# Spectral layers on one core: the place of an older group's inverse, and of its copy, in the middle stage

## The chip, the cores and the metric

The kernel runs on one core of a Trainium2 chip. The metric is the device time of one execution in microseconds (us), over several runs: before the change the median of three is 1185.11 us (1184.79 to 1185.26). The profile shows one further execution.

The engines are named as in the profile: PE is TensorE (PEld is its loading of weights), ACT is ScalarE, DVE is VectorE, POOL is GpSimd, SP is SyncE. ACTq and SPq are the queues from which an engine issues DMAs.

## The reference

A row of 2048 positions by 576 channels goes through four layers. Layers A are Fourier mixing: layer norm, a DFT over the channels and one over the sequence, the real part of it, and a residual. Layers B are an H3 block: layer norm, then a gate that is a long causal convolution along the sequence, done by FFT for each channel.

```
def A(x): a, b = x @ Wd_re.T, x @ Wd_im.T          # 576 x 576
          return Ws_re @ a - Ws_im @ b              # 2048 x 2048
def B(q): kv = shift_conv(k, 4 taps) * v
          y = irfft(rfft(kv, 4096) * rfft(ssm_k, 4096))[:2048] + kv * ssm_D
          return q * y
x = x + A(norm(x)); x = x + B(norm(x)); x = x + A(norm(x)); x = x + B(norm(x))
```

The convolution `y` doesn't depend on `x`, so the kernel computes it once and uses it in both B layers.

## The kernel before, in words

Matrices are held as two float32r parts, a high and a low one, and a product is three matmuls: high by high, high by low, low by high. What splits a value into its parts is a copy on ScalarE (the high part, rounded) and a subtraction on VectorE (the low part).

*The two halves of the first 600 us.* The first A layer is the function `layer`: 128 steps, of 14 matmuls of 512 columns each ("s" and "rm" in the profile, four full accumulators and one for the remaining columns), over a matrix of which 128x512 pieces arrive by DMA and are split (lines 99 and 100, "mats"). When two groups of 16 steps are done, the four or five accumulators are copied out (`evac_u`, `evac_r`), and the product with the channel DFT follows for four row blocks (`hidden`, "bk<-w,u": blocks of 27 matmuls of 288 columns; VectorE adds the result to the residual at line 289). The convolution is a generator, `branch`, that is woven in between these matmuls. It has a first stage (the outer part of the FFT), the **middle stage** with which the change deals, and a last one (`i2_products`, the outer part of the inverse FFT).

*The middle stage.* There are 64 groups (two channel halves by 32). For group g:

- `mid_kernel` (line 522): three matmuls of 288 columns, the "kernel trio", into a bank; then three ScalarE copies (lines 524 to 526) that lay out the kernel's spectrum in one of two tiles `kk`.
- `mid_signal` (529): the "signal trio" into a bank; then VectorE's lines 532 to 535 make the complex product with the spectrum, in place, in the `kk` tile.
- `mid_round` (538): the product is split into `yf` (two tiles), a rounding on ScalarE and a subtraction on VectorE (line 520, 128x288).
- `mid_inverse` (543): the "inverse trio" from `yf` into a bank, ScalarE's copy of it (549) and the store to memory (550).
- `split_feed(i + 2)` (588): the split of the feed two places ahead (ScalarE, line 514 in the profile, 128x576; VectorE, line 520), and `load_feed`, the DMA of a later one.

The trios use three PSUM banks in rotation ("bk"), which the hidden blocks and the output products use as well. All ScalarE work of the stage goes through `act` (511), which chains each instruction to the one before it: ScalarE does it in the order of the source. In the profile its line is 514, and that of the low halves 520. The copies and subtractions for the DFT matrix pieces may stand between.

*What sets the order.* `branch` yields numbers, the cost that it claims for what it has just issued. The loop at line 792 calls it as long as its claims stay behind a share of what the layer has done (`spent < work * passed / total`, line 816); each step of the layer and each hidden block adds to `passed`. A scheduler then places the instructions of all engines, by the order of the source and by its own reckoning of what is ready.

In the loop over the feeds (602 to 646) a group before is: the inverse of an older group if `yfs` holds two, 0.4, the kernel of g, the rounding of g-1, 1.6, the signal of g, the feed split and load, 1.1. From group 37 on an output product (`kind` 1) comes after every second group.

Of the kernel before, what the change touches and what calls it, by code (L numbers as in the profile page):

```python
# [39 lines left out]
MID_FROM = 47  # L40
I2_END = 111
PREP = 113
MID_LAG = 2
BORDER = {J - 1: 0.5, 0: 0.75}
I2_FIRST = 37
I2_LATE = 6
I2_COST = 2.0
# [19 lines left out]
def fnet_h3_kernel(ctx: ExitStack, tc: tile.TileContext, x, c_mat, w_re, w_im, k_pad, v, shift_k,  # L67
# [7 lines left out]
    def mm(ps, lhsT, rhs, first, last, more=False):  # L75
        return nc.tensor.matmul(ps, lhsT, rhs, start=first, stop=last, skip_group_check=more).ins  # L76
# [7 lines left out]
    def bank():  # L84
        return psp.tile([P, NT], F32, tag="b", bufs=3, name="bk")
# [46 lines left out]
    def lay(t, at, *sizes):  # L132

        for name, words, n in sizes:
            ring.setdefault(name, Ring()).tiles.extend(t[:, at + i * words:at + (i + 1) * words] for i in range(n))
            at += n * words
        assert at <= t.shape[1], (at, t.shape, sizes)
        return at

    def fresh(*names):  # L140
        for name in names:
            ring[name] = Ring()

    def two(v):
        return v.rearrange("p (a n) -> p a n", a=2)
# [205 lines left out]
    def branch():  # L351
# [150 lines left out]
        def mid_half(df, o):  # L502
            ps = bank()
            mm(ps[:, :HD], mc[:, 0, :], df[0][:, o:o + HD], True, False)
            mm(ps[:, :HD], mc[:, 0, :], df[1][:, o:o + HD], False, False)
            mm(ps[:, :HD], mc[:, 1, :], df[0][:, o:o + HD], False, True)
            return ps
# [3 lines left out]
        def act(*args, **kw):  # L511
            if last_act:
                with tc.issue_after(last_act[-1]):
                    last_act.append(nc.scalar.activation(*args, **kw).ins)  # L514
            else:
                last_act.append(nc.scalar.activation(*args, **kw).ins)
# [5 lines left out]
        def mid_kernel(df):  # L522
            pk, kk = mid_half(df, HD), two(ring["kk"]())
            act(kk[:, 0, :], pk[:, :HD], AF.Copy)
            act(kk[hi, 1, :], kk[hi, 0, :], AF.Copy)
            act(kk[hi, 0, :], kk[lo, 0, :], AF.Copy)
            return kk

        def mid_signal(df, kk):
            px = mid_half(df, 0)  # L530
            p1, p2 = kk[:, 0, :], kk[:, 1, :]
            nc.vector.scalar_tensor_tensor(p2[lo], px[hi, :HD], -1.0, p2[hi], op0=OP.mult, op1=OP.mult)  # L532
            nc.vector.tensor_tensor(p2[hi], px[lo, :HD], p2[hi], OP.mult)  # L533
            nc.vector.tensor_tensor(p1, px[:, :HD], p1, OP.mult)  # L534
            nc.vector.tensor_tensor(p1, p1, p2, OP.add)  # L535
            return p1

        def mid_round(p1):
            yf = two(ring["yf"]())
            act_split(yf[:, 0, :], yf[:, 1, :], p1)  # L540
            return yf

        def mid_inverse(hf, qg, yf):
            pv = bank()
            mm(pv[:, :HD], mc[:, 2, :], yf[:, 0, :], True, False)
            mm(pv[:, :HD], mc[:, 2, :], yf[:, 1, :], False, False)
            mm(pv[:, :HD], mc[:, 3, :], yf[:, 0, :], False, True)
            vo = ring["vo"]()
            act(vo, pv[:, :HD], AF.Copy)
            nc.scalar.dma_start(v_d[hf][4 * qg:4 * qg + 4].rearrange("m j d -> (m j) d"), vo)  # L550

        def i2_products(hf, j, fc, vf):
            yo = ring["vo"]()
            ps = [bank() for _ in range(2)]
            for i in range(2):
                cs = slice(i * HD, (i + 1) * HD)
                mm(ps[i][:, :HD], fc[:, i, :], vf[0][:, cs], True, False)
                mm(ps[i][:, :HD], fc[:, i, :], vf[1][:, cs], False, True)
            for i, (main, corr) in enumerate(((lo, hi), (hi, lo))):
                act(yo[main], ps[i][main, :HD], AF.Copy)  # L560
                nc.vector.tensor_tensor(yo[main], ps[i][corr, :HD], yo[main], OP.add)
                nc.sync.dma_start(yb_d[j][i::2, hf * HD:(hf + 1) * HD], yo[main])
# [11 lines left out]
        landed, halves, fcs, yfs = {}, {}, {}, []  # L574

        def load_feed(i):
            if i < len(feeds):
                kind, hf, q = feeds[i]
                landed[i] = ring["land"]()
                load_after(two(landed[i]) if kind else landed[i], v_d[hf][:, q::J, :] if kind else  # L580
                           t_d[4 * q:4 * q + 4, :, hf * D:(hf + 1) * D].rearrange("m j d -> (m j) d"))

        def load_fc(k):
            if k < len(rows):
                fcs[k] = two(ring["fc"]())
                load_fr(fcs[k], i2c[rows[k]])

        def split_feed(i):
            if i < len(feeds):
                halves[i] = parts("df")  # L590
                act_split(*halves[i], landed.pop(i))
# [9 lines left out]
        used, ahead, feed_ahead, product = 0, 2, 3, None  # L601
        for i, (kind, hf, q) in enumerate(feeds):
            df = halves.pop(i)
            if kind:
                i2_products(hf, q, fcs.pop(used), df)
                load_fc(used + ahead)
                used += 1
            else:
                if len(yfs) == MID_LAG:
                    mid_inverse(*yfs.pop(0))  # L610
                    yield 0.4
                kk = mid_kernel(df)
                if product is not None:
                    yfs.append((*product[:2], mid_round(product[2])))
                yield 1.6
                product = hf, q, mid_signal(df, kk)
            split_feed(i + 2)
            if i >= I2_FIRST - 8 and feed_ahead == 3:
                tiles = [ring["land"]() for _ in range(3)]
                if tiles[0] is third:  # L620
                    ring["land"], feed_ahead = Ring(tiles[1:]), 2
                    lay(m1, fc_at, ("fc", 2 * P, 2))
                    load_fc(0)
                    load_fc(1)
            if feed_ahead == 2:
                feed_ahead = 2.5
            else:
                load_feed(i + int(feed_ahead) + 2)
            if i == last_mid:
                yield 0.4  # L630
                mid_inverse(*yfs.pop(0))
                yfs.append((*product[:2], mid_round(product[2])))
                while yfs:
                    yield 0.4
                    mid_inverse(*yfs.pop(0))
                for name, t, at, words in (("fc", m1, spare, 2 * P), ("land", flts, kk_at, D)):
                    old = ring[name]
                    held = [old.tiles[(old.n + m) % 2] for m in range(2)]
                    fresh(name)
                    lay(t, at, (name, words, 2))  # L640
                    ring[name].tiles.extend(held)
                for m in range(2):
                    load_fc(used + ahead + m)
                    load_feed(i + ahead + 3 + m)
                ahead = feed_ahead = 4
            yield I2_COST if kind else 1.1

    def sums(src, junk):
        m = ring["stat"]()
# [115 lines left out]
    pending = []  # L765
    lay(flts, SC_AT, ("craw", NT, CRAW))
    br = branch()
    wl = load_w()
    load_x(0)
# [405 lines left out]
```

## Time and profile before

| | |
|---|---|
| median of 3 runs | 1185.11 us (1184.79 to 1185.26) |
| the profiled execution | 1183.61 us |
| its span, first to last instruction | 1181.8 us |
| granted TensorE clock | 0.999 |
| middle stage's trios on TensorE | 211.5 to 540 us, the output products to 598 us |

The page of the profile gives the busy time of each engine and the chain that ended last. The table of waits gives, for an engine, for whom it waited, how long in total, how often, and the longest. A row of the timeline is the start in us, the length in us, the engine, the line, the operation, what it writes and reads ("<-"), the shape and the count, and at the end in brackets how long the engine had been idle and who released it. A row of a window gives the span, then for each engine its busy us and its number of instructions, the clock, and the DMA share. A row of instruction groups gives the busy time, the mean of one in ns, and the idle time ahead of them by releaser.

### The profile page before, as it was taken

What the parts mean: (1) busy time and instruction counts of PE and PEld (TensorE: products, weight loads), DVE (VectorE), ACT (ScalarE), POOL (GpSimd) and SP (SyncE); (2) the same over time, 40 slices, a digit from 0 to 9 for tenths busy, and PEclk for the clock granted to TensorE, in tenths of its full rate; (3) what the DMA queues carried; (4) which work ended last, traced back from release to release, by engine and by line L of the source; (5) the groups of instructions that cost most, each with busy time, mean ns of one, the idle gap of its engine ahead of it and who ended that gap; (6) DMA issues with size and microseconds to landing.
All of it is one profiled execution on the core that took longest, in us unless ns stands there. A gap on an engine that the chain in (4) does not pass through costs nothing.

```text
span 1181.8 us, 18082 instructions
## 1 busy us (share of the span) xinstructions
PE 1167.8 (99%) x6198; PEld 989.1 (84%) x6198; DVE 868.6 (73%) x1564; ACT 650.8 (55%) x1280; POOL 75.5 (6%) x115
## 2 busy tenths in 40 slices
PE   8999999999999999999999999999999999999997
PEld 6776667988888888888888898888888888889997
DVE  7899983788877778787756765865776777774764
ACT  8865655577766667766645666534444445550210
POOL 2310000000000000001101111000000000001111
PEclk9999999999999999999999999999999999999999
DMA  9879898546666656648966777762872787894621
GB/s 336 284 232 316 263 300 272 160 152 173 213 214 193 203 168 193 190 140 247 270 192 215 249 240 231 247 253 73 257 249 72 221 284 258 260 338 144 219 93 40
DMA packets 147453, 255.64 MB, mean 216 GB/s; under 512 B 16161, under 2 KB 56353, under 8 KB 147362
## 3 DMA queue, kind: packets, MB, share of 16 engines
q1 hardware_dynamic: 111890, 210.17, 55.6%
q10 hardware_dynamic: 28560, 37.91, 9.2%
q0 software_dynamic: 6912, 6.43, 2.5%
q8 instruction: 48, 0.79, 0.3%
q14 instruction: 43, 0.35, 0.1%
HBM read 187.80 MB, written 66.65 MB: 215 GB/s over the span
## 4 chain that ended last, share of the span: by engine, by line
PE 77%; ACT 2%; DVE 2%; DMA 1%; issue 1%; ACTq 0%; DVEq 0%
PE s L76 43%; PE bk L76 30%; PE rm L76 4%; ACT flts L514 1%; ACT mid L514 1%; DVE mid L520 0%; DMA flts<-td 0%; DMA flts<-in_c_mat 0%; ACT mats L99 0%; DVE flts L534 0%; DVE flts L533 0%; DVE flts L532 0%; DVE flts L535 0%; ACTq L550 0%; ACT u L99 0%
## 5 line engine op out<-in xcount | busy, mean ns | idle before, releaser
L76 PE MATMUL s<-mats 128*128 128x512 f32 x2102 | 545.9, 395 | 4.2 <-ACT mats L197 2.4
L76 PEld LDWEIGHTS s<-mats 128*128 128x128 f32 x2102 | 382.7, 188 | 86.1 <-issue 10.9
L100 DVE TENSOR_TENSOR mats<-flts,mats 128x512 fp32r<-128x512 f32 x206 | 140.6, 686 | 50.3 <-ACT mats L99 48.9
L99 ACT ACTIVATE mats<-flts 128x512 fp32r<-128x512 f32 x206 | 128.2, 627 | 81.8 <-PE bk L76 30.7
L76 PE MATMUL bk<-mid 128*128 128x288 f32 x704 | 126.7, 300 | 2.1 <-DVE flts L289 0.8
L76 PEld LDWEIGHTS bk<-mid 128*128 128x128 f32 x704 | 108.6, 188 | 23.0 <-ACT flts L514 5.9
L514 ACT ACTIVATE flts<-bk 128x288 f32<-128x288 f32 (+1 forms) x192 | 76.5, 405 | 90.4 <-PE bk L76 71.6
L76 PE MATMUL bk<-w,u 128*128 128x288 f32 x864 | 120.6, 295 | 0.4 <-DVE w L243 0.4
L76 PEld LDWEIGHTS bk<-w,u 128*128 128x128 f32 x864 | 117.4, 188 | 3.5 <-ACT flts L514 0.9
L520 DVE TENSOR_TENSOR mid<-flts,mid 128x576 fp32r<-128x576 f32 (+1 forms) x149 | 93.3, 627 | 19.1 <-ACT mid L514 16.4
L76 PE MATMUL rm<-mats 128*128 128x512 f32 x304 | 94.5, 390 | 0.2 <-ACT flts L514 0.2
L514 ACT ACTIVATE mid<-flts 128x576 fp32r<-128x576 f32 (+1 forms) x148 | 80.5, 576 | 10.3 <-DVE flts L535 5.1
L289 DVE TENSOR_TENSOR flts<-flts,bk 128x288 f32<-128x288 f32 x48 | 21.8, 453 | 68.3 <-PE bk L76 65.9
L76 PE MATMUL bk<-mats 128*128 128x288 f32 (+1 forms) x376 | 67.8, 317 | 0.0
L76 PEld LDWEIGHTS rm<-mats 128*128 128x128 f32 x304 | 56.9, 188 | 12.6 <-ACT flts L514 0.6
L453 ACT ACTIVATE flts<-bf 128x384 f32<-128x384 f32 (+1 forms) x104 | 43.2, 462 | 43.4 <-PE bf L76 43.2
L76 PE MATMUL s<-t,mats 128*128 128x512 f32 x264 | 64.9, 389 | 0.0
L186 POOL TENSOR_TENSOR flts<-flts 128x1 f32<-128x1 f32 x34 | 28.0, 823 | 515.6 <-DVE flts L185 513.2
L76 PE MATMUL bk<-mats,t 128*128 128x288 f32 (+1 forms) x368 | 59.3, 303 | 0.0
L514 ACT ACTIVATE flts<-flts 64x288 f32<-64x288 f32 x128 | 56.6, 443 | 4.5
L76 PEld LDWEIGHTS bk<-mats 128*128 128x128 f32 x376 | 55.6, 188 | 3.4
L76 PEld LDWEIGHTS s<-t,mats 128*128 128x128 f32 x264 | 49.6, 188 | 10.3
(152 smaller groups left out, 1495.0 us busy)
## 6 DMA issues: line engine op xcount, KB each, us to landing
flts<-in_c_mat SPq DMA_DIRECT2D x148, 256.0 KB, 3.5
ph<-in_c_mat SPq DMA_DIRECT2D x54, 512.0 KB, 4.0
flts<-in_c_mat SPq DMA_DIRECT2D x30, 512.0 KB, 5.2
flts<-td SPq DMA_DIRECT2D x53, 288.0 KB, 3.1
td<-flts ACTq DMA_DIRECT2D x36, 384.0 KB, 4.2
vd<-flts ACTq DMA_DIRECT2D x64, 144.0 KB, 2.3
flts<-vd SPq DMA_DIRECT2D x32, 288.0 KB, 4.1
ud<-ph ACTq DMA_DIRECT2D x12, 512.0 KB, 6.7
```

Of the source, the lines that this page charges most:

```text
L76: return nc.tensor.matmul(ps, lhsT, rhs, start=first, stop=last, skip_group_check=more).ins
L99: a = nc.scalar.activation(h, src, AF.Copy).ins
L100: return a, nc.vector.tensor_tensor(l, src, h.bitcast(F32), OP.subtract).ins
L186: pows.append(nc.gpsimd.tensor_tensor(rs, ve, mhalf, OP.pow).ins)
L289: added[:] = [nc.vector.tensor_tensor(r[:, cs], r[:, cs], ps[:, :HD], OP.add).ins]
L453: stored[:] = [nc.scalar.activation(so[:, i, :], ps[i], AF.Copy).ins]
L514: last_act.append(nc.scalar.activation(*args, **kw).ins)
L520: nc.vector.tensor_tensor(l, src, h.bitcast(F32), OP.subtract)
```

## The change

It moves the inverse. A group becomes: the kernel of g, 1.6, the signal of g, and, if `yfs` holds one, 1.1 and the inverse of that group; then the rounding of g-1, the feed split and load, 0.4. As the rounding of g-1 is added to `yfs` only after the older one was taken out, the inverse at the end of group g is that of g-2; before, the one at the start of group g was that of g-3. ScalarE's chain before is: the inverse's copy, the kernel's three copies, the rounding, the feed split. After, it is: the kernel's three copies, the inverse's copy, the rounding, the feed split. At the end of the stage one inverse less is left over.

```
-MID_LAG = 2
+MID_LAG = 1
...
             else:
+                kk = mid_kernel(df)
+                yield 1.6
+                p1 = mid_signal(df, kk)
                 if len(yfs) == MID_LAG:
+                    yield 1.1
                     mid_inverse(*yfs.pop(0))
-                    yield 0.4
-                kk = mid_kernel(df)
                 if product is not None:
                     yfs.append((*product[:2], mid_round(product[2])))
-                yield 1.6
-                product = hf, q, mid_signal(df, kk)
+                product = hf, q, p1
             split_feed(i + 2)
...
             if i == last_mid:
-                yield 0.4
-                mid_inverse(*yfs.pop(0))
                 yfs.append((*product[:2], mid_round(product[2])))
                 while yfs:
                     yield 0.4
...
-            yield I2_COST if kind else 1.1
+            yield I2_COST if kind else 0.4
```

## The prediction, made before the changed kernel ran

> **What bounds the kernel now.** I read the page's shares first, then the wait table of TensorE's weight loader over the middle stage, then the order in which the two built programs place their instructions, then one burst of the stage in the timeline.
>
> ```profile
> PE 1167.8 (99%) x6198; PEld 989.1 (84%) x6198; DVE 868.6 (73%) x1564; ACT 650.8 (55%) x1280; POOL 75.5 (6%) x115
> PE 77%; ACT 2%; DVE 2%; DMA 1%; issue 1%; ACTq 0%; DVEq 0%
> 213.00:600.00 387.00, 385.24 (x2192) 337.86 (x2193) 303.00 (x590) 266.30 (x566) 16.88 (x32) 1.00 0.64 193
> 750.00:780.00 30.00, 30.00 (x135) 24.83 (x133) 22.49 (x38) 12.97 (x23) 0.00 (x0) 1.00 0.70 231
> ```
>
> TensorE is busy 99% of the span, and 77% of the chain that ended last is its work. All matmuls stay, so only time in which TensorE stands still can change. The built programs' matmul orders agree for the first 1058 and the last 3004 of 6198; they differ only over about 212 to 600 us, the third row. Elsewhere nothing can happen.
>
> The loader's share there is 338 of 387 us (87%). [...]
>
> ```profile
> PEld bk L76 <- ACT flts L514: 6.8, 21, 0.9
> PEld bk L76 <- DVE mid L520: 1.5, 5, 0.4
> PEld bk L76 <- DVE flts L534: 1.4, 4, 0.6
> PEld bk L76 <- DVE flts L289: 1.2, 1, 1.2
> PEld bk L76 <- ACT mid L514: 1.1, 3, 0.5
> PEld bk L76 <- DVE flts L561: 0.9, 4, 0.4
> PEld rm L76 <- ACT flts L514: 0.6, 1, 0.6
> PEld bk L76 <- issue: 0.4, 1, 0.4
> ```
>
> That is the loader over 213 to 600 us: 40 waits, 13.9 us. Half is one row: 21 waits, 6.8 us, for ScalarE's copies at line 514, which free the three rotating banks. What such a wait costs is seen in one burst (start, length, engine):
>
> ```profile
> 347.97 1.66 PEld L76 LDWEIGHTS bk<-mid 128*128 128x128 f32 x12
> 348.10 1.77 PE L76 MATMUL bk<-mid 128*128 128x288 f32 x12
> 348.30 0.45 DVE L289 TENSOR_TENSOR flts<-flts,bk 128x288 f32<-128x288 f32 x1 [2.38 <-PE bk L76]
> 348.70 0.41 ACT L514 ACTIVATE flts<-bk 128x288 f32<-128x288 f32 x1 [3.59 <-PE bk L76]
> 349.14 0.92 ACT L514 ACTIVATE flts<-flts 64x288 f32<-64x288 f32 x2
> 349.62 0.46 DVE L532 SCALAR_TENSOR_TENSOR flts<-bk,flts 64x288 f32<-64x288 f32 x1 [0.86 <-ACT flts L514]
> 349.71 1.77 PE L76 MATMUL s<-mats 128*128 128x512 f32 x7
> 350.08 1.02 ACT L514 ACTIVATE mid<-flts 128x288 fp32r<-128x288 f32 x2
> 350.97 0.45 DVE L534 TENSOR_TENSOR flts<-bk,flts 128x288 f32<-128x288 f32 x1
> 351.01 0.69 ACT L514 ACTIVATE flts<-bk 128x288 f32<-128x288 f32 x2
> 351.45 0.43 PEld L76 LDWEIGHTS bk<-mid 128*128 128x128 f32 x3 [0.40 <-ACT flts L514]
> 351.45 0.67 PE L76 MATMUL bk<-mid 128*128 128x288 f32 x3
> 352.42 0.56 PE L76 MATMUL bk<-mid 128*128 128x288 f32 x3
> ```
>
> A block of the hidden product ends at 348.10. Kernel 29, signal 29, inverse 27 and kernel 30 run at once (12 matmuls). ScalarE copies kernel 29 (three copies), does the two roundings (350.08, 1.02 us), and only then, at 351.01, copies inverse 27 out, ready since about 349.5. Signal 30 wants that bank, and starts at 351.45. The last of the seven matmuls before it started at 349.71 + 1.77 - 0.39 = 351.09, and one follows another by (1.77 - 0.39)/6 = 0.23, so 0.13 is lost; then the trio takes 0.67 in place of 0.56, 0.11 more. A loader wait of 0.40 costs TensorE 0.25: the wait less 0.15. The 40 waits are worth about 13.9 - 6.0 = **7.9 us**: no change here can gain more.
>
> **The change part by part.** *TensorE.* Before, the inverse at the start of group g is that of g-3; after, the one at the end of g is that of g-2. The last trio of group g and the first of g+1 meet, so the cyclic order of trios is the same: inverse, kernel, signal. The paces between them (0.4, 1.6, 1.1) are the same too. No matmul is added; cost 0. But the first groups, before inverses begin, now take 2.0 of pace rather than 2.7, and two such groups stand there rather than three: all later groups come up to 1.5 pace units earlier against the hidden blocks. That re-deals which trios crowd behind a block.
>
> *ScalarE.* Same instructions, another order: inverse copy, rounding, feed split, then the next kernel's three copies. The copy no longer stands behind the roundings; so the waits of signals for an inverse's bank go. The built program names the instruction of each wait; these are the five in the first row here (213 to 250 us), three of the five in the second (250 to 340), the five in the third (340 to 425), and three of the four in the last (425 to 455).
>
> ```profile
> PEld bk L76 <- ACT flts L514: 0.9, 5, 0.2
> PEld bk L76 <- ACT flts L514: 1.3, 5, 0.5
> PEld bk L76 <- ACT flts L514: 2.0, 5, 0.4
> PEld bk L76 <- ACT flts L514: 2.2, 4, 0.9
> ```
>
> With 0.9 of the second row and 1.9 of the last, that makes 16 waits and 5.7 us, less 16 x 0.15: **3.3 us saved**. The lone wait of the rm bank, 0.6, goes as well: the evacuation of that bank then stands ahead of its first use by more than a microsecond. Saved 0.45.
>
> *What is late next.* The roundings now come after a copy that waits for TensorE, and the inverse g-1 needs the rounding's high half (ScalarE) and low half (VectorE). In an undisturbed group this is hidden:
>
> ```profile
> L514 ACT ACTIVATE flts<-bk 128x288 f32<-128x288 f32 x128 | 50.6, 406 | 68.5 <-PE bk L76 54.3 <-ACT flts L514 6.0 <-DVE mid L520 4.3
> L514 ACT ACTIVATE flts<-flts 64x288 f32<-64x288 f32 x128 | 56.6, 443 | 4.5
> L514 ACT ACTIVATE mid<-flts 128x288 fp32r<-128x288 f32 x64 | 28.5, 445 | 6.6 <-DVE flts L535 5.1
> L514 ACT ACTIVATE mid<-flts 128x576 fp32r<-128x576 f32 x83 | 56.1, 676 | 3.7 <-DMA flts<-td 3.1
> L520 DVE TENSOR_TENSOR mid<-flts,mid 128x288 fp32r<-128x288 f32 x64 | 29.3, 458 | 16.2 <-ACT mid L514 14.8
> L520 DVE TENSOR_TENSOR mid<-flts,mid 128x576 fp32r<-128x576 f32 x85 | 64.0, 754 | 2.9 <-ACT mid L514 1.6
> 298.75 0.46 DVE L532 SCALAR_TENSOR_TENSOR flts<-bk,flts 64x288 f32<-64x288 f32 x1
> 303.12 0.46 DVE L532 SCALAR_TENSOR_TENSOR flts<-bk,flts 64x288 f32<-64x288 f32 x1
> ```
>
> A group lasts 4.37 us (last two rows). After an inverse ends, ScalarE needs 0.2 to see it (348.50 to 348.70 above), then 0.41 + 0.45 + 0.68 + 0.41 + 0.89 = 2.84: it is through at 3.0 of 4.37. The rounding is used a whole group later. The feed load that follows the split on SP's queue keeps its distance of two groups to its use, and the store of the inverse, which the new order puts behind the kernel's copy on ScalarE's queue, is read many groups later. Cost 0; without that cover each group would pay.
>
> In a burst it isn't hidden. Take block 8 of the changed order: signal 26, inverse 24, kernel 27, one s matmul, signal 27, two s, inverse 25, two s, kernel 28 with one s inside. From the block's end, at 0.134 a short and 0.23 a long matmul: inverse 24 ends at 0.80, kernel 27 at 1.21, signal 27 wants to start at 1.44, the low half of inverse 25 is wanted at 2.43, that of kernel 28 at 3.52. ScalarE: copy 1.00 to 1.41, rounding to 1.86, split to 2.53. VectorE: hidden add to 0.65, three products of 0.46 to 2.03, low half of the rounding to 2.49, the last sum to 2.95, low half of the split to 3.70. So signal 27 finds its bank free within 0.05 (with the two roundings still in front it would wait 1.1); inverse 25 is about 0.1 late, kernel 28 about 0.2, and each wait has its 0.11 for the next load. Between 0 (all three just in time) and 0.6 a burst; I take **0.3**, by this working. Blocks 8 to 11, 14, 16 and 17 have this form: +2.1. In groups 3 to 13 the same half-late roundings and splits fall seven times, by the same steps 0.15 each: +1.0 (0 to 2). In the crowded stretch at 425 to 455, where bank evacuations and output products share ScalarE, the waits other than the three saved stay, and two copies there get later by a rounding: +0.4 (-0.5 to 1).
>
> Sum: -3.3 - 0.45 + 2.1 + 1.0 + 0.4 = **-0.3 us**. The profiled execution took 1183.61 us (span 1181.8 and 1.8 around it), 1.5 below the median of the three runs, 1185.11; the difference is put on the median: **1184.8**.
>
> **The rivals.** *The copies' waits go and nothing takes their place.* For it: in the burst above the new waits are 0.05 to 0.2, within what these rows resolve, and an inverse's rounding has two thirds of a group in the ordinary case. Then -3.3 - 0.45 + 0.4: about -3.4, 1181.7.
>
> *The roundings become the wait* (slower). ScalarE works in order, and the table above has 54.3 us in which its bank copies wait for TensorE; half of these copies now have the roundings behind them. [...] Place: the inverse and the kernel right behind a burst, whose low halves stand on VectorE behind three products of a signal. Price: 0.6 for each of ten bursts and 0.3 for each of seven early ones, +8.1, less 3.75: +4.4, 1189.5; from about 0.3 a burst above my estimate (0.6 rather than 0.3) it makes the change slower by over 0.2%. Against it: the VectorE chain of the burst was worked out with no idle time left in it, and gives 0.3.
>
> *A loop through the ring of two kernel tiles* (slower). A kernel's copy must wait until the low half of an older rounding has read the tile; that low half now stands behind three products, which wait for the previous kernel's copies. Loop: 0.41 + 0.44 + 3 x 0.46 + 0.69 (a split of the DFT matrix between) + 0.46 and about 0.3 of hand-overs = 3.7 us against 4.37. It decides from 4.37; 0.1 beyond that costs some 45 undisturbed groups 4.5 us, less 3.75: +0.8 and up.
>
> *The change does not do what it says*: no other inverse is taken, only ScalarE's order and the phase against the hidden blocks change, and the phase re-deals stalls of equal size. That is inside my forecast.
>
> **How the numbers follow.** 0.2% of the median is 2.4 us; a measurement of this kernel can tell about that from no change. Forecast, gains and new waits nearly even: 0.51, its own range 1182.8 to 1187.4. Nothing in place of the waits: 0.24. Roundings late: 0.18. Loop: 0.07. Faster 0.24, within 0.2% 0.51, slower 0.25. The range reaches from the saved waits alone (1181.7) to two thirds of the way to the late roundings: **1181.6 to 1188.0**.
>
> **What would show it.** Right: in the wait table of 213 to 600 us the row for bank copies of line 514 falls from 6.8 to about 2, the rows for VectorE's and ScalarE's mid tiles (1.5 and 1.1) rise to 2 to 4 together, and the group stays at 4.37. The first rival: those rows don't rise. The second: they rise above 6. The loop: the spacing of line 532 between blocks exceeds 4.4. I am wrong in kind if TensorE's count outside 212 to 600 us changes, or if a wait for a feed's DMA appears on the loader's path.

## The result, and the profile after

The changed kernel takes **1186.4 us** (median of 16 runs, 1184.84 to 1188.12), the kernel before, run beside it, **1183.72 us** (16 runs, 1181.9 to 1186.7). The ratio is 1.0020, 95% interval 1.0014 to 1.0027: **2.4 us slower**, where I forecast 0.3 us faster. The time lies inside the range, on the wrong side. The profiled execution has a span of 1185.3 us, 3.5 over that of before.

The page's first line and the chain of the changed kernel, then the loader's waits over 213 to 600 us:

```profile
PE 1169.0 (99%) x6198; PEld 990.7 (84%) x6198; DVE 866.7 (73%) x1564; ACT 647.8 (55%) x1280; POOL 75.5 (6%) x115
PE 78%; DVE 1%; DMA 1%; ACT 1%; issue 0%; DVEq 0%; ACTq 0%; SPq 0%
```
```profile
PEld bk L76 <- ACT flts L514: 7.4, 20, 2.7
PEld bk L76 <- DVE mid L520: 1.4, 6, 0.4
...
PEld rm L76 <- PE s L76: 0.9, 1, 0.9
PEld bk L76 <- ACT mid L514: 0.8, 3, 0.3
PEld bk L76 <- DVE flts L534: 0.4, 1, 0.4
```

The page's shares are the same as before and show nothing. In the waits the third number, the longest, tells most. The row of bank copies is 7.4 where 6.8 stood, but one wait of 2.7 is in it; the other 19 come to 4.7. The two rows of mid tiles stand at 1.4 and 0.8 where 1.5 and 1.1 stood: the roundings did not become late.

To place the loss I added up, matmul by matmul, by how much each started later after the one before than the usual 0.223 us (512 columns) or 0.131 (288). The matmuls from 1058 to 3193, the stretch of the middle stage, lose 16.7 us before and 20.0 after. Matmuls 1200 to 1500 (240 to 298 us) lose 2.3 before and **7.3** after; the rest of the stretch loses 14.4 before and 12.8 after. So the change loses 4.9 us in one place and gains 1.6 outside it. The gain stands in one place too: matmuls 2200 to 2600 (421 to 496 us) lose 1.8 less than before, and what is left is even within 0.5. The place of the loss in the timeline of the changed kernel, loader, then matmuls, and then four windows:

```profile
273.79 0.60 PEld L76 LDWEIGHTS bk<-mid 128*128 128x128 f32 x3 [2.75 <-ACT flts L514]
```
```profile
270.62 0.85 PE L76 MATMUL s<-mats 128*128 128x512 f32 x3
273.80 0.94 PE L76 MATMUL bk<-mid 128*128 128x288 f32 x3 [2.32 <-ACT flts L514]
274.54 1.05 PE L76 MATMUL s<-mats 128*128 128x512 f32 x2
275.39 1.05 PE L76 MATMUL rm<-mats 128*128 128x512 f32 x2
```
```profile
273.00:274.00 1.00, 0.20 (x1) 0.21 (x2) 0.93 (x3) 0.98 (x4) 0.00 (x0) 1.00 0.00 0
274.00:275.00 1.00, 1.00 (x5) 0.91 (x5) 0.97 (x4) 0.65 (x2) 0.00 (x0) 0.50 0.86 201
277.00:278.00 1.00, 1.00 (x5) 0.81 (x5) 0.89 (x3) 0.93 (x3) 0.00 (x0) 0.80 0.74 226
278.00:279.00 1.00, 1.00 (x8) 0.87 (x7) 0.97 (x3) 1.00 (x3) 0.00 (x0) 1.00 0.44 141
```

Signal 13 waits for the bank of inverse 10. Three matmuls start at 270.62, so the next could have started at 270.62 + 3 x 0.223 = 271.29; it starts at 273.80, 2.5 us late. **Then the matmuls run at half speed**: two of 512 columns in 1.05 us where three take 0.85, and the granted clock (the third number from the end) is 0.50 until 277.4. By the same count this costs 1.7 us more. A shorter stop, 0.6 us, stands ahead of it at 261.

Of the 16 executions nine show a mean clock of 0.997 (their mean is 1187.1 us), six 0.999 (1185.4 us). The half clock thus seems to come in about half of the executions and to cost 1.7 us there; the stop by itself leaves the change 1.7 slower. One execution alone has a trace with the half clock in it; for the others this is inferred from the mean clock.

**Where the stop comes from**, followed backwards. ScalarE of the changed kernel:

```profile
256.54 0.41 ACT L514 ACTIVATE flts<-bk 128x288 f32<-128x288 f32 x1
...
256.99 0.33 ACTq L550 DMA_DIRECT2D vd<-flts  x1
...
260.29 0.59 ACT L274 ACTIVATE flts<-rm 64x512 f32<-64x512 f32 x1 [0.65 <-DMA vd<-flts]
...
263.50 0.62 ACT L99 ACTIVATE mats<-flts 128x512 fp32r<-128x512 f32 x1
...
271.74 0.63 ACT L99 ACTIVATE mats<-flts 128x512 fp32r<-128x512 f32 x1 [2.14 <-DMA flts<-in_c_mat]
272.40 0.91 ACT L514 ACTIVATE flts<-flts 64x288 f32<-64x288 f32 x2
273.33 0.41 ACT L514 ACTIVATE flts<-bk 128x288 f32<-128x288 f32 x1
```

The last line is inverse 10's copy. It comes behind the kernel's copies (272.40), and these behind the split of a piece of the DFT matrix, piece 53, which waits 2.14 us for its DMA. That DMA is issued at 266.57, the first of the two in the row of SP's queue, and lands at 271.66, 5.1 us later (the row behind it is VectorE's low half of piece 51, which frees the raw tile that piece 53 is loaded into):

```profile
266.57 2.67 SPq L169 DMA_DIRECT2D flts<-in_c_mat  x2
```
```profile
265.86 0.68 DVE L100 TENSOR_TENSOR mats<-flts,mats 128x512 fp32r<-128x512 f32 x1
```

Piece 51's tile in its turn waits for step 48's matmuls into the rm bank, which wait for line 274, the evacuation of step 47: it runs at 260.29, though that bank's last matmul began at 251.68. It waits **for a store of the middle stage** ("DMA vd<-flts"). The reason is memory: the scratch tile that line 274 writes lies at words 5376 to 5888 behind `SC_AT` (a place in the kernel's tile `flts`), the fourth of the `vo` tiles, from which an inverse is stored, at 5344 to 5632. Inverse 7 uses that tile, and in the changed program its copy (256.54) and its store (256.99) come ahead of the evacuation. The row of the kernel before shows the order the other way round (inverse 7's copy, waiting for the evacuation's split):

```profile
254.57 0.59 ACT L274 ACTIVATE flts<-rm 64x512 f32<-64x512 f32 x1
...
260.32 0.71 ACT L514 ACTIVATE flts<-bk 128x288 f32<-128x288 f32 x2 [1.69 <-DVE u L100]
```

And there piece 53 is issued at 261.51, five us earlier, as the second of the two in this row, and lands at 264.44, after 2.9 us:

```profile
260.91 0.94 SPq L169 DMA_DIRECT2D flts<-in_c_mat  x2
```

### The profile page after: what moved, and what is told of

The parts are those of the page before. It is cut to its first block, busy times and chain, and to the rows that moved or that the text cites. A ratio compares the mean times of both kernels' runs of the same rounds, so it can differ in the third digit from the quotient of the medians.

```text
span 1185.3 us, 18120 instructions
## 1 busy us (share of the span) xinstructions
PE 1169.0 (99%) x6198; PEld 990.7 (84%) x6198; DVE 866.7 (73%) x1564; ACT 647.8 (55%) x1280; POOL 75.5 (6%) x115
## 4 chain that ended last, share of the span: by engine, by line
PE 78%; DVE 1%; DMA 1%; ACT 1%; issue 0%; DVEq 0%; ACTq 0%; SPq 0%
PE s L76 44%; PE bk L76 29%; PE rm L76 4%; DMA flts<-in_c_mat 1%; ACT flts L514 1%; DMA yb<-flts 0%; DMA vd<-flts 0%; DVE mid L520 0%; ACT mid L514 0%; DVE u L100 0%; DVE flts L532 0%; ACT u L99 0%; DVE mats L100 0%; DVE flts L534 0%; DVE flts L533 0%
## 5 line engine op out<-in xcount | busy, mean ns | idle before, releaser
L76 PE MATMUL bk<-mid 128*128 128x288 f32 x704 | 132.8, 303 | 3.5 <-ACT flts L514 2.3
L76 PEld LDWEIGHTS bk<-mid 128*128 128x128 f32 x704 | 111.5, 189 | 25.3 <-ACT flts L514 6.8
L76 PEld LDWEIGHTS rm<-mats 128*128 128x128 f32 x304 | 57.3, 189 | 12.8 <-PE s L76 0.9
```

## The experiments

The theory to be tested: one event makes the loss. Its head is that the phase, not the order, puts inverse 7's copy in front of the evacuation. Rivals: the new order itself costs (roundings late); the piece is late because of SP's queue. All ratios are to the kernel before, run on the same chip.

**1. New order, old phase.**

```
-            yield I2_COST if kind else 0.4
+            yield I2_COST if kind else 0.4 if i > 1 else 1.1
```

> The changed order, but the two groups that run before inverses begin claim 2.7 again (1.1 at their end, not 0.4), so every later group stands where it stood before the change. Theory (one event): the loss is a single stop of TensorE of about 2.5 us at 271 us plus a stretch at half clock behind it, and it comes from the phase: with the groups earlier, inverse 7's copy stands ahead of line 274's evacuation of the rm bank, whose scratch tile shares memory with the fourth output tile, so the evacuation waits for that copy's store. With the old phase the evacuation stands ahead of inverse 6 again: no stop, and the rest of the change is left, 3.5 us of span less about 5.3 for the event: 1 to 2 us faster than the kernel before. Rival (the new order itself, roundings late at every burst): about 2.4 us slower than before here too, spread over many waits.

Measured: 1182.7 us against 1185.12, ratio **0.9979 (0.9969 to 0.9989): 2.5 us faster**. Loader waits, 213 to 600 us:

```profile
PEld bk L76 <- ACT flts L514: 5.0, 16, 0.6
PEld bk L76 <- DVE flts L534: 1.7, 5, 0.6
...
PEld bk L76 <- DVE mid L520: 1.0, 3, 0.4
PEld bk L76 <- ACT mid L514: 1.0, 3, 0.3
```
```profile
253.42 0.59 ACT L274 ACTIVATE flts<-rm 64x512 f32<-64x512 f32 x1
...
268.00 0.62 ACT L99 ACTIVATE mats<-flts 128x512 fp32r<-128x512 f32 x1
```

No wait is over 1.2; the evacuation runs at 253.42, and piece 53's split (268.00) waits for nothing. The rival of the late roundings falls: with the same order the kernel is faster. This is also the fastest version found.

**2. Old order, new phase.**

```
-            yield I2_COST if kind else 1.1
+            yield I2_COST if kind else 1.1 if i > 1 else 0.4
```

> The order of before, but the two groups ahead of the first inverses claim 2.0, so every later group comes earlier, as in the changed kernel. Theory (one event from the phase): in the built program the evacuation of the rm bank stands behind inverse 7's copy and waits for its store here too, so a stop of TensorE of 0.5 to 3 us appears between 255 and 280 us, and the kernel is 1 to 5 us slower than before. Rival (the new order itself): within 1 us of before, no stop of over 1 us.

Measured: 1185.82 against 1185.12, 1.0007 (0.9997 to 1.0017), +0.8 us, which isn't clear of no change. The stop is there in the old order as well:

```profile
259.90 0.60 ACT L274 ACTIVATE flts<-rm 64x512 f32<-64x512 f32 x1 [0.30 <-DMA vd<-flts]
```
```profile
272.54 0.43 PEld L76 LDWEIGHTS bk<-mid 128*128 128x128 f32 x3 [1.77 <-ACT flts L514]
```

It is shorter, the clock stays at 1.00 behind it (272 to 282 us), and the total is a little under what the theory gave (1 to 5). Phase and order don't seem to add up: in the old phase the new order is worth -2.5, in the new one about +1.6 (2.4 - 0.8, each with about 1 us of uncertainty).

**3 and 4. Three output tiles**, so that none shares memory with the scratch tile; in the changed kernel (3), and in the kernel before (4).

```
-        lay(flts, at, ("land", D, 2), ("kk", D, 2), ("vo", HD, 4))
+        lay(flts, at, ("land", D, 2), ("kk", D, 2), ("vo", HD, 3))
...
             if i == last_mid:
+                lay(flts, kk_at + 2 * D + 3 * HD, ("vo", HD, 1))
```

> The changed kernel with three output tiles in the middle stage instead of four (the fourth comes back after the last group), so that none shares memory with the scratch tile of line 274. Theory (the store of inverse 7 through shared memory): line 274 runs as soon as the rm bank is done, the stop at 271 us and the half clock go, 1 to 2.5 us faster than the kernel before. Rival (the DFT matrix piece is late because the feed's load stands ahead of it on SP's queue): the stop stays, about 2 us slower than before. Rival (the new order itself): about 2 us slower, with no single stop.

> The kernel before with three output tiles. In before the same memory makes inverse 7's copy wait 1.69 us on ScalarE for the evacuation's split, with no stop of TensorE behind it. Theory: within 1 us of before, either way (the waits of line 514, 6.8 us in all, stay). If it gains 1 us or more, the shared memory cost the kernel before as well.

Measured: (3) 1184.03, 0.9990 (0.9980 to 1.0000), 1.2 us faster than before; (4) 1185.64, 1.0004 (0.9994 to 1.0014). In (3) the evacuation runs at 252.39, no store in front of it, and the half clock is gone (1.00 over 260 to 290 us), but not the whole stop; (4) even has a stop that the kernel before hasn't:

```profile
270.12 0.43 PEld L76 LDWEIGHTS bk<-mid 128*128 128x128 f32 x3 [0.94 <-ACT flts L514]
```
```profile
272.08 0.43 PEld L76 LDWEIGHTS bk<-mid 128*128 128x128 f32 x3 [1.13 <-ACT flts L514]
```

The shared memory is thus a large part of the event, not all of it: a stop of this kind also comes without it.

**5. The copy back behind the roundings**, in the old phase.

```
+                rounded_yf = mid_round(product[2]) if product is not None else None
+                split_feed(i + 2)
                 if len(yfs) == MID_LAG:
                     yield 1.1
                     mid_inverse(*yfs.pop(0))
                 if product is not None:
-                    yfs.append((*product[:2], mid_round(product[2])))
+                    yfs.append((*product[:2], rounded_yf))
```

> The inverse stays at the end of the group, with the phase of before, but the rounding and the feed split are issued ahead of it, so that its copy stands behind ScalarE's two roundings as it did before the change. Theory (what is gained with the old phase, 2.4 us, is the copy's place in front of the roundings): the gain goes, within 1.2 us of the kernel before, and the row of bank copies of line 514 is back from 5.0 to 6 or more. Rival (the gain comes from the inverse at the end, or from being the younger one): still 2 us faster than before.

Measured: 1183.95 against 1184.82, 0.9993 (0.9985 to 1.0001), -0.8 us. About 1.7 us of the 2.5 go, as the theory has it, but not through the row it named:

```profile
PEld bk L76 <- DVE flts L534: 3.6, 10, 0.6
PEld bk L76 <- ACT flts L514: 3.5, 16, 0.4
```

Bank copies cost less than in experiment 1 (3.5 to 5.0), and the products of line 534, which free a signal's bank, twice as much (3.6 to 1.7). That part of the expectation was wrong.

**6 and 7. The feed loads on GpSimd's queue**, in the changed kernel (6), and with three output tiles (7).

```
-                load_after(two(landed[i]) if kind else landed[i], ...
+                (load_after if kind else load_fr)(two(landed[i]) if kind else landed[i], ...
```

> The changed kernel as it is, but the feed loads of the middle stage go through GpSimd's queue, so that no DFT matrix piece stands behind a feed on SP's queue. Theory (the stop at 271 us comes from the evacuation's wait for a store): the piece's load still waits for its raw tile, which the late evacuation frees late; a stop of 1.5 to 3 us stays near 271 us and the kernel is 1 to 3 us slower than before. Rival (the piece is late because the feed's load stands ahead of it): the stop falls below 0.7 us, and the kernel is 0.5 to 2.5 us faster than before.

> The changed kernel with three output tiles and the feed loads on GpSimd's queue. With three tiles alone a wait of 0.94 us was left near 270 us, where two matrix pieces were issued at 264.5, behind a feed's load at 263.5. If the rest is the order on SP's queue, that wait goes and the kernel is 0.5 to 1 us faster than with three tiles alone: 1.5 to 2.5 us faster than before. If it is something else (the time at which the raw tiles come free), no change: 1 us faster than before.

Measured: (6) 1184.78 against 1184.82, 1.0000 (0.9991 to 1.0010); (7) 1183.80, 0.9995 (0.9985 to 1.0006). (6), loader:

```profile
272.29 0.43 PEld L76 LDWEIGHTS bk<-mid 128*128 128x128 f32 x3 [1.85 <-ACT flts L514]
```

The stop stays, but shorter by 0.9 us than in the changed kernel and without the half clock (1.00 over 270 to 280), and the kernel is level with before, not 1 to 3 us slower: 2.4 less than the changed kernel lost. Taking the feeds off SP's queue thus helps, by an amount that neither theory had. It isn't the issue that they held up (see the table below): piece 53 follows its free tile as closely as in the changed kernel, but lands 4.2 us after its issue, not 5.1. In (7) the wait near 270 us stays (1.16): what is left with three tiles isn't SP's queue.

**8 and 11. Forced stops**, in the kernel before: an inverse's copy done again n times, and the layer's next matmul behind the signal that waits.

```
-            act(vo, pv[:, :HD], AF.Copy)
+            for _ in range(1 + more):
+                act(vo, pv[:, :HD], AF.Copy)
...
+                if hf == 0 and q in (16, 20, 24):
+                    forced[:] = tail
...
-                mm(ps[dc], xh, c[0], first, False)
+                with behind(*forced):
+                    mm(ps[dc], xh, c[0], first, False)
```

> The kernel before with three stops of TensorE made on purpose in a quiet stretch: the copy of an inverse is done 12, 15 and 18 times over in groups 15, 19 and 23, which makes the kernel copies and products behind it late, and the layer's next matmul may not be issued ahead of the signal that waits. Estimated stops 1.5, 2.5 and 3.5 us, at about 285, 303 and 320 us. To be read: for which of them the matmuls behind run at half clock, and for how long. From the changed kernel's stop: half clock for about 3.5 us, 1.7 to 2.2 us lost, behind stops of 2.3 us and more; none behind the shorter one.

> The kernel before with three forced stops of TensorE in groups 16, 20 and 24, by 13, 17 and 21 extra copies of an inverse, and with every later matmul of the layer behind the waiting signal. In the first try the stops came out at 0.8 to 0.95 us and no clock fell. Estimated stops 1.5, 2.7 and 3.9 us. To be read: the clock behind each. From the changed kernel: full clock behind the 1.5, half clock for about 3.5 us behind the longest, the middle one open.

Experiment 8 failed as a test: the scheduler put other matmuls in the gaps, and its waits are 0.83, 0.95 and 0.83 (one execution, 1189.4 us). Experiment 11 (one execution, 1204.9 us) gave stops in pairs. Its matmuls around the first and second pair and behind the first stop of the third, then three windows behind the second:

```profile
284.32 1.06 PE L76 MATMUL bk<-mid 128*128 128x288 f32 x6 [0.38 <-ACT flts L515]
285.22 1.15 PE L76 MATMUL rm<-mats 128*128 128x512 f32 x4
287.42 0.66 PE L76 MATMUL bk<-mid 128*128 128x288 f32 x3 [1.05 <-ACT flts L515]
...
307.36 1.06 PE L76 MATMUL bk<-mid 128*128 128x288 f32 x6 [1.72 <-ACT flts L515]
310.02 1.09 PE L76 MATMUL bk<-mid 128*128 128x288 f32 x3 [1.59 <-ACT flts L515]
...
333.75 2.93 PE L76 MATMUL rm<-mats 128*128 128x512 f32 x6 [2.75 <-DVE flts L275]
```
```profile
308.00:310.00 2.00, 0.42 (x4) 0.19 (x2) 1.75 (x5) 1.94 (x6) 0.00 (x0) 0.78 0.23 74
312.00:314.00 2.00, 2.00 (x7) 1.61 (x7) 1.97 (x5) 0.32 (x1) 0.00 (x0) 0.50 0.35 122
316.00:318.00 2.00, 2.00 (x11) 1.70 (x11) 0.54 (x2) 1.70 (x5) 0.00 (x0) 1.00 0.22 73
```

With idle times of 0.38 and 1.05 the clock is 1.00 (280 to 300 us); with 1.72 and 1.59 within 4.4 us it is halved from 309.1 to 315.9, with 2.75 and a later 0.83 from 333.0 to 343.2. As the stops came in pairs, the estimated single ones weren't tried.

**9 and 10. Other phases of the new order**: half of the shift (9), and a shift to the other side (10).

```
-            yield I2_COST if kind else 0.4
+            yield I2_COST if kind else 0.4 if i > 0 else 1.1     # 9
+            yield I2_COST if kind else 0.4 if i > 1 else 1.8     # 10
```

> The changed order with only the first of the two groups ahead of the inverses claiming 2.7: half of the phase shift. In the built program the evacuation of the rm bank (line 274) still stands behind inverse 7's copy on ScalarE and waits for its store. Theory (the place of the evacuation against that copy decides, not the size of the shift): a stop of 1 to 3 us between 265 and 280 us, and 0 to 3 us slower than before. Rival (the loss grows with the shift): halfway between the changed kernel and the one with the old phase, no change from before, with no stop of over 1 us.

> The changed order with both groups ahead of the inverses claiming 3.4, so that every later group comes 1.4 of the claims later than before. In the built program the evacuation stands right ahead of inverse 7's copy. Theory: no stop of over 1 us near 271 us, and 1 to 3 us faster than before, like the old phase. Rival (any phase other than that of before loses): 1 us or more slower than before.

Measured: (9) 1183.81 against 1184.42, 0.9990 (0.9978 to 1.0001); (10) 1184.39, 0.9994 (0.9986 to 1.0003). (9) contradicts my theory's head; no change and no stop of over 1 us there is what the rival gave. Its evacuation waits for the store for longer than in the changed kernel, and no loader wait of over 0.71 us follows within 30 us:

```profile
260.41 0.60 ACT L274 ACTIVATE flts<-rm 64x512 f32<-64x512 f32 x1 [2.21 <-DMA vd<-flts]
...
267.02 0.63 ACT L99 ACTIVATE mats<-flts 128x512 fp32r<-128x512 f32 x1
```

Here VectorE does piece 51's low half right behind its split, at 263.37, not behind four operations of a group; piece 53 is issued at 264.09, and its split (267.02) has no wait. But the same thing happens to this kernel, in the profiled execution, 190 us later: ScalarE, loader, and the window behind:

```profile
457.14 0.63 ACT L99 ACTIVATE mats<-flts 128x512 fp32r<-128x512 f32 x1 [2.12 <-DMA flts<-in_c_mat]
```
```profile
460.01 0.40 PEld L76 LDWEIGHTS bk<-mid 128*128 128x128 f32 x2 [2.26 <-DVE flts L534]
```
```profile
460.00:464.00 4.00, 3.98 (x11) 3.24 (x12) 3.16 (x6) 2.06 (x5) 0.53 (x1) 0.57 0.44 136
```

A split that waits for its DMA in ScalarE's line, a stop of 1.9 us on TensorE (its waits came from 458.1 to 460.0), a granted clock of 0.57 over the four us behind it: the class of the event is a late piece of the matrix, whatever made it late. (10) has no stop near 271, as expected, but gains 0.7 us rather than 1 to 3, not clear of no change, and isn't slower, as the rival had it: two waits of 1.08 and 0.75 come at 546 and 557 us.

**12. Piece 53's high part on GpSimd**, in the changed kernel.

```
-            halved[:] = split(t[0], t[1], raw)
+            halved[:] = (split_pool if step in ((1, 1, 5),) else split)(t[0], t[1], raw)
...
+    def split_pool(h, l, src):
+        a = nc.gpsimd.tensor_copy(h, src).ins
+        return a, nc.vector.tensor_tensor(l, src, h.bitcast(F32), OP.subtract).ins
```

> The changed kernel with one instruction moved: the high part of DFT matrix piece 53, whose DMA lands at 271.7 us, is made by GpSimd rather than ScalarE; its low part stays on VectorE. The built program keeps TensorE's order but for a few matmuls at that place. Theory (the stop comes from the bank copies that stand behind this one split on ScalarE): the wait of 2.75 us falls below 1, no half clock behind it, and the kernel is 0.5 to 3 us faster than before. Rival (the piece itself is needed, or VectorE's work behind it): the stop stays above 1.5 us and the kernel is 1 to 3 us slower than before.

Measured: 1185.88 against 1184.42, **1.0015 (1.0005 to 1.0026): still slower**. Signal 13 no longer waits, but a stop comes a little later. VectorE, then the matmuls:

```profile
273.65 0.69 DVE L104 TENSOR_TENSOR mats<-flts,mats 128x512 fp32r<-128x512 f32 x1 [1.94 <-POOL mats L103]
```
```profile
275.46 0.81 PE L76 MATMUL bk<-mid 128*128 128x288 f32 x3 [1.53 <-DVE flts L538]
```

The low half of the late piece now holds VectorE's line, and with it the products that free the signal's bank. My theory had ScalarE's line alone; the rival was right. What helps is to have the piece earlier, as in experiment 1 and, in part, in 3.

**All traces side by side.** The time at which piece 53's load is issued and has landed (two traces don't record the landing), and the largest gap that TensorE lost between 262 and 282 us, from the profiled execution of each (matmul 1058, with which the stage begins, differs by up to 1.7 us between them):

| kernel | evacuation of step 47 | piece 53 issued | landed | largest gap |
|---|---|---|---|---|
| 10 later phase | 254.76 | 259.88 | - | 0.07 |
| 1 new order, old phase | 253.42 | 260.29 | - | 0.01 |
| before | 254.57 | 261.51 | 264.44 | 0.07 |
| 5 copy behind roundings | 255.14 | 262.77 | 265.60 | 0.06 |
| 7 three tiles, feeds on GpSimd | 251.57 | 263.72 | 267.42 | 0.90 |
| 9 half phase | 260.41 | 264.09 | 266.65 | 0.43 |
| 3 three tiles | 252.39 | 264.49 | 267.98 | 0.68 |
| 4 old order, three tiles | 255.37 | 264.93 | 268.74 | 0.87 |
| 2 old order, new phase | 259.90 | 265.45 | 269.50 | 1.51 |
| 6 feeds on GpSimd | 259.66 | 265.95 | 270.15 | 1.58 |
| changed kernel | 260.29 | 266.57 | 271.66 | 2.49 |

In experiment 12, with the piece off ScalarE, it is issued at 267.66, lands at 272.85, and 1.69 is lost. Up to about 263 nothing is lost; from there the loss grows with the lateness (the 0.43 of (9) comes at 265.4, ahead of this piece).

Two things make the piece late. The first is its issue. In every one of these traces the load is issued within 0.1 us of the end of piece 51's low half on VectorE (266.54 in the changed kernel, 261.49 before), so it waits for its raw tile, and not for a feed ahead of it on SP's queue. A late evacuation goes with the worst three, but (9) shows that it isn't enough: where VectorE's low half stands decides the rest. In (3) and (7) the split of piece 51 is early (258.35 and 257.54), but VectorE does its low half 5.4 us later, behind operations of the groups.

The second is the transfer. It takes 2.6 to 3.8 us in the traces that issue it before 265 and 4.1 to 5.2 in the later ones. In the changed kernel this makes up the whole wait of 2.14 us on ScalarE: with the 2.93 us of before the piece would have landed at 269.50, ahead of 269.60, when ScalarE came free. By an estimate from these rows the inverse's copy would then have ended at 271.60, not 273.74, and the stop would have been 0.4 us, not 2.5. The late piece of (9) at 457 took 5.66 us. Why these transfers are slow is open: in the changed kernel a feed issued at 265.60 and a store issued at 266.34 are under way with the piece, and take 5.03 and 4.69 us. How the store's wait and VectorE's place share the five us of the issue is not settled one by one either.

## Why the prediction was wrong

- **The step that failed** is "the change part by part", where moved loads and stores were put at nothing: "The feed load that follows the split on SP's queue keeps its distance of two groups to its use, and the store of the inverse ... is read many groups later. Cost 0". It followed each to its reader, and asked neither for whom it stands in the queue nor who needs the memory behind the store. In their place the runs showed: the store holds line 274's scratch tile, and a matrix piece behind it is issued 5 us and lands 7 us later than before; without the feeds on SP's queue the loss is 2.4 us less. Cost in the profiled execution: 2.5 us of stop, 0.6 at 261 us, and 1.7 of half clock, against a term of zero.
- **The phase** was seen ("re-deals which trios crowd behind a block") and priced only against the hidden blocks. The layer's own step, where a bank is evacuated and matrix pieces are split, was left out. With the old phase the same order gains 2.5. That the time fell inside the range is luck: its upper end stood for late roundings, which did not come.
- **Waits saved** (3.3 and 0.45): the row of bank copies fell to 4.7 apart from the one wait (about 2 forecast). The rm bank's wait at 326 us went, and one of 0.9 came at 261.
- **New waits in bursts** (+2.1) and early groups (+1.0) were too large. Experiment 1 against before, by lost time per stretch: matmuls 1058 to 1800 (to 349 us) -0.3, 1800 to 2200 (to 417) +0.3, 2200 to 2600 (to 492) **-1.75**, the rest -0.5. My sum by the same stretches was about 0, +0.9, -1.1, 0. The copies' waits in bursts were nearly traded for others, as said; the gain is the crowded stretch, where I had taken off 0.4 and should have added. One burst of the changed kernel behind a block that ends at 354.50:

```profile
355.49 0.41 ACT L514 ACTIVATE flts<-bk 128x288 f32<-128x288 f32 x1 [3.71 <-PE bk L76]
355.80 0.44 ACT L514 ACTIVATE mid<-flts 128x288 fp32r<-128x288 f32 x1
355.95 0.43 PEld L76 LDWEIGHTS bk<-mid 128*128 128x128 f32 x3 [0.18 <-ACT flts L514]
```

  The inverse's copy stands ahead of the rounding, and the signal waits 0.18 where it waited 0.40.
- **The rivals.** "Roundings become the wait" named the right side with the wrong mechanism: its rows (mid tiles) didn't rise, and the group stayed at 4.39 us (line 532 at 312.18 and 316.57). "Nothing takes their place" (-3.4) is near to what the order does in the old phase (-2.5). "I am wrong in kind if ... a wait for a feed's DMA appears" came close: it was the DMA of a matrix piece, which is none of the stage's own.

## What to carry to other kernels

When a step moves, go through every queue that it crosses and ask what else stands there, and which memory its stores keep busy, at the one or two places where another loop turns over; averages over the steady groups don't show it. A change of order should be tried with the phase held still, and a change of phase by itself: here they were -2.5 and +0.8 us apart and +2.4 together. The largest single wait in the "longest" column is worth reading ahead of the totals.

## What the runs showed of the hardware

In two profiled executions a stop of TensorE cost more than its length. In the changed kernel, behind a lost gap of 2.49 us that ends at 273.80, the granted clock was 0.50 from 273.99 to 277.41, 3.4 us. In experiment 9, behind one of 2.10 (460.02, less 457.70 and one matmul of 0.22), it was 0.57 over 460 to 464 us, which is 3.4 us if it was 0.50, and 1.00 over 464 to 470. Behind gaps of 1.51 (experiment 2, 272 to 282 us), 1.58 (experiment 6, 270 to 290) and 1.69 (experiment 12, 270 to 290) it stayed at 1.00.

In experiment 11, one execution, the clock fell at 309.1, within the second of two stops with idle times of 1.72 and 1.59 us, and at 333.0, within one of 2.75. At what length of a stop the clock falls, these runs don't settle. For the executions without a trace there is the mean clock alone: of the 16 of the changed kernel nine, the profiled one among them, have 0.997 and six 0.999.
